# States and first batch loaded in F32 and cast on chip, attention one batch ahead, state rows inside the last batch

## The chip, the cores and the metric

The kernel runs on one core of a Trainium2 chip. A core has five engines that run their own instruction queues: TensorE (PE, with its weight loads shown as PEld), VectorE (DVE), ScalarE (ACT), GpSimd (POOL) and SyncE (SP). They meet only at semaphores, and 16 DMA engines move data between HBM and the on-chip memory. The metric is device time in microseconds of one execution of the whole program; lower is better.

## The reference

For each of 8 batches and 8 heads, 512 tokens `x` attend to 32 state rows, and the state rows attend back to the tokens. The two results are joined along the token axis (544 rows per batch), heads are put side by side into rows of 512, and a feed-forward layer with a maximum over three projections follows.

```python
scores = scale * np.matmul(x, state.transpose(0, 1, 3, 2))
a = softmax(scores)                      # over the 32 states
xread = np.matmul(a, state)              # (8, 8, 512, 64)
scores2 = scale * np.matmul(state, x.transpose(0, 1, 3, 2))
a2 = softmax(scores2)                    # over the 512 tokens
sread = np.matmul(a2, x)                 # (8, 8, 32, 64)
x = np.concatenate([xread, sread], axis=2).transpose(0, 2, 1, 3).reshape(4352, 512)
h = np.maximum(np.maximum(x @ w1, x @ w2), x @ w3)   # 512 -> 768
out = h @ w_out                                       # 768 -> 512
```

All inputs and the output are F32. The kernel computes its matmuls in bf16.

## The kernel before

Everything is unrolled and the order is written by hand: each engine executes its instructions in the order in which the source issues them, and the framework adds the semaphore waits from the tiles that are read and written. Buffers with a tag are shared: of the PSUM tag "two" (two banks each) there are two, of "pw" (one bank each) four.

Start. POOL issues all loads, and each of them casts F32 to bf16 on the way: the states (`st_sb`, two DMAs, L61), x of batch 0 (L71), six pieces of w1, w2, w3 (L81; half c=0 of the columns of all three, then half c=1), x of batches 1 and 2, `wout` (L91), and x of batches 3 to 7. The states are transposed on PE (L109) and copied into `bd` (L114 on DVE, L115 on ACT), where each head's transposed state lies once in the upper and once in the lower 64 partitions beside zeros, so that one matmul serves two token groups.

Attention of one batch is four pieces.

- `xt_piece` transposes x on PE into PSUM (`pxt`, L127) in two groups of eight, with a DVE copy to `xT` after each group (L130).
- `score_piece` multiplies with `bd` (`ps`, L136); ACT takes the exponential `e` (L141); DVE sums it (`den`, L143) and inverts (`rden`, L145); POOL multiplies to get the attention `a` (L147).
- `sread_piece` forms the state rows on PE (`psr`, L157 and L164) and normalises them on DVE (`rd`, `ats`, L170 and L171).
- `at_piece` transposes `a` on PE (`pat`, L180), copied by DVE to `aT` (L184).

The token rows never form xread. Instead `g_piece(b, u)`, for six u, multiplies the states of batch b with a sixth of the columns of w1, w2, w3 (`pg`, L197), and ACT casts the result to `G` (L202). `x_maxout(b, m)`, for six m of 128 hidden columns, multiplies `G` with `aT`: three projections of two matmuls each into three `pw` buffers (L212). ACT casts the first (`t0`, L216), DVE takes the two maxima (`t1`, L217; `ht`, L218). For m 0 to 2 it reads the columns of u 0 to 2, for m 3 to 5 those of u 3 to 5. `s_maxout(m)` does the same for the state rows of all batches, directly from the weights. `ffn_out(b, jj)` multiplies half of the tokens of `ht` with `wout` (`po`, 12 matmuls, L238), ACT copies to `osb` (L241), SP stores it (L248; the state rows in eight DMAs, L245).

Order. Attention of batch 0, its six g pieces, attention of batch 1. Then a loop over b, with six slots m: `x_maxout(b, m)` first, and after it what the slot holds. Slots 0, 2, 4, 5 hold the four attention pieces of batch b+2, slots 1 and 3 the two `ffn_out` of batch b-1, and every slot one g piece of batch b+1. After the loop come the six `s_maxout`, with the two `ffn_out` of batch 7 after the second and the fourth, and last the `ffn_out` of the state rows.

## Time and profile before

| | us |
|---|---|
| median of 3 runs | 213.42 (212.78 to 214.81) |
| profiled execution, device time | 215.94 |
| its span, first to last instruction | 214.1 |
| PE busy | 168.2 (79%) |
| DVE busy | 109.2 (51%) |
| ACT busy | 90.8 (42%) |
| POOL busy | 30.3 (14%) |
| PE weight loads (beside PE) | 87.9 (41%) |

The profile is of one execution. A group row gives the line, the engine, the operation, output and inputs by the program's names, the shapes, the count, then the busy time in us and the mean duration in ns, then the idle time of that engine just before and what ended it. A timeline row gives start and duration in us, engine, line and names, and in brackets how long the engine had been idle before and what released it. The chain that ended last is followed back from the last instruction, at each step to what released it; its rows are start, duration and piece. A DMA issue row gives the count, the size of one and the median time from issue to landing. Busy shares are means over stages with different limits, so the stretches of the span are to be read one by one. A run of matmuls is pipelined: the duration of a row holds the drain of the last one, so six matmuls of 512 columns show 1.47 us although the next instruction can start before that.

### The profile page before, as it was taken

To read this page: it belongs to the slowest core of one execution; us is meant where nothing else is said; L and a number is where in the kernel's file an instruction comes from. 1 tells how busy PE (TensorE), PEld (TensorE's weight loads), DVE (VectorE), ACT (ScalarE), POOL (GpSimd) and SP (SyncE) were. 2 spreads that over 40 slices of the span, in tenths; PEclk is the share of its full clock that TensorE was granted. 3 is DMA by queue.
4 is the path that set the end of the run, shared out by engine and by line. 5 is a ranking of instruction groups with operands and counts; after the bars stand their busy time and mean duration, and the time that the engine had idled before them with its cause. 6 is when DMAs were issued, how large, how long until landed. Compare 5 with 4: busy or idle time off the path is not lost.

```text
span 214.1 us, 3798 instructions
## 1 busy us (share of the span) xinstructions
PE 168.2 (79%) x1581; PEld 87.9 (41%) x1604; DVE 109.2 (51%) x170; ACT 90.8 (42%) x131; POOL 30.3 (14%) x31
## 2 busy tenths in 40 slices
PE   0452275589969996998799699978999999999970
PEld 0341125344434453444344344444444334456630
DVE  3334014456972776359645943595459338443330
ACT  2310081126544662654285327542865654342320
POOL 7944500300300300030003000300030000000000
PEclk9999999999999999999999969999999999999995
DMA  6999999910000120201022002100220210220223
GB/s 45 158 199 203 199 203 198 198 26 0 3 0 31 71 98 3 99 36 65 0 101 98 0 3 98 79 22 2 101 98 3 98 74 24 98 101 2 98 98 98
DMA packets 17056, 16.75 MB, mean 78 GB/s; under 512 B 2704, under 2 KB 14736, under 8 KB 17040
## 3 DMA queue, kind: packets, MB, share of 16 engines
q0 software_dynamic: 14352, 7.60, 26.0%
q1 hardware_dynamic: 2688, 8.91, 10.5%
q8 instruction: 12, 0.20, 0.4%
q14 instruction: 4, 0.03, 0.0%
HBM read 15.20 MB, written 8.91 MB: 113 GB/s over the span
## 4 chain that ended last, share of the span: by engine, by line
PE 50%; DVE 17%; ACT 9%; issue 8%; DMA 6%; POOL 5%; another core or an unknown queue 2%; DVEq 0%; ACTq 0%; POOLq 0%
PE pw L212 21%; PE po L238 20%; DVE t L217 6%; DMA w<-in_moe_w_dram 6%; DVE ht L218 4%; ACT G L202 4%; PE pg L197 3%; PE pxt L127 3%; ACT t L216 2%; DVE xT L130 2%; DVE rd L170 2%; POOL a L147 2%; PE ps L136 2%; ACT osb L241 2%
## 5 line engine op out<-in xcount | busy, mean ns | idle before, releaser
L212 PE MATMUL pw<-aT,G 128*128 128x512 bf16 x269 | 72.2, 395 | 2.7 <-issue 1.1
L217 DVE TENSOR_TENSOR t<-t,pw 128x512 bf16<-128x512 bf16 (+1 forms) x54 | 35.0, 648 | 56.1 <-ACT t L216 49.7
L202 ACT CAST G<-pg 128x768 bf16<-128x768 f32 x48 | 38.1, 801 | 46.0 <-PE pg L197 46.0
L238 PE MATMUL po<-wout,ht 128*128 128x512 bf16 x200 | 47.0, 383 | 0.2
L212 PEld LDWEIGHTS <-G 128*128 128x128 bf16 x288 | 25.4, 100 | 34.9 <-issue 13.1
L218 DVE TENSOR_TENSOR ht<-t,pw 128x512 bf16<-128x512 bf16 (+1 forms) x54 | 35.5, 658 | 5.6
L241 ACT COPY osb<-po 128x1024 f32<-128x1024 f32 x17 | 17.2, 1012 | 45.8 <-PE po L238 42.9
L216 ACT CAST t<-pw 128x512 bf16<-128x512 f32 (+1 forms) x54 | 31.0, 574 | 9.9 <-PE pw L212 9.8
L147 POOL TENSOR_TENSOR a<-e,rden 128x1024 bf16<-128x1024 bf16 x8 | 15.3, 1912 | 118.7 <-DVE rden L145 118.7
L238 PEld LDWEIGHTS <-ht 128*128 128x128 bf16 x204 | 20.2, 99 | 24.2 <-issue 1.3
L127 PE MATMUL pxt<-ident,x 128*128 128x128 bf16 x128 | 12.2, 252 | 13.0 <-DVE xT L130 11.1
L197 PE MATMUL pg<-w,bd 64*32 64x384 bf16 x384 | 18.3, 357 | 2.8 <-DVE ats L171 1.6
L130 DVE COPY xT<-pxt 128x1024 bf16<-128x1024 bf16 x16 | 11.0, 689 | 13.7 <-PE pxt L127 13.7
L127 PEld LDWEIGHTS <-x 128*128 128x128 bf16 x128 | 10.2, 114 | 16.4 <-issue 13.1
L180 PE MATMUL pat<-ident,a 128*128 128x128 bf16 x64 | 5.7, 242 | 10.4 <-POOL a L147 10.4
L197 PEld LDWEIGHTS <-bd 64*32 64x32 bf16 x384 | 5.9, 90 | 15.0 <-issue 13.0
L141 ACT ACTIVATE e<-ps 128x1024 bf16<-128x1024 f32 x8 | 8.2, 1023 | 8.8 <-PE ps L136 8.7
L143 DVE TENSOR_REDUCE den<-e 128x32 f32<-128x1024 bf16 x8 | 9.7, 1215 | 4.1 <-ACT e L141 3.9
L184 DVE COPY aT<-pat 128x1024 bf16<-128x1024 bf16 x8 | 5.5, 686 | 9.9 <-PE pat L180 9.9
L180 PEld LDWEIGHTS <-a 128*128 128x128 bf16 x64 | 4.7, 109 | 12.3 <-POOL a L147 10.9
L212 PE MATMUL pw<-ats,w 128*128 128x256 bf16 x72 | 8.5, 273 | 0.0
L71 POOL DMA_DIRECT2D x<-in_x_dram x8 | 7.1, 884 | 6.4 <-DMA w<-in_moe_w_dram 5.9
(29 smaller groups left out, 68.6 us busy)
## 6 DMA issues: line engine op xcount, KB each, us to landing
out_dram<-osb SPq DMA_DIRECT2D x16, 512.0 KB, 2.6
x<-in_x_dram POOLq DMA_DIRECT2D x8, 512.0 KB, 20.2
w<-in_moe_w_dram POOLq DMA_DIRECT2D x6, 384.0 KB, 10.5
wout<-in_moe_w_out_dram POOLq DMA_DIRECT2D x1, 768.0 KB, 19.0
out_dram<-osb SPq DMA_DIRECT2D x8, 64.0 KB, 1.7
st<-in_state_dram POOLq DMA_DIRECT2D x2, 128.0 KB, 3.7
```

What stands on the lines that cost most here:

```text
L127: nc.tensor.transpose(pxt[:, h, jj, :], x_sb[b][:, h, 2 * jj:2 * jj + 2, :].rearrange("p j d -> p (j d)"), ident)
L130: nc.vector.tensor_copy(out=xT[b][:, 4 * g:4 * g + 4], in_=pxt[:, 4 * g:4 * g + 4])
L147: nc.gpsimd.tensor_mul(out=a[b].rearrange("p j h n -> p (j h) n"), in0=e[b].rearrange("p j h n -> p (j h) n"), in1=rden.rearrange("p j h - ...
L180: nc.tensor.transpose(pat[:, q * 512 + j * 128:q * 512 + j * 128 + 128], a[b][:, j, 4 * q:4 * q + 4, :].rearrange("p h n -> p (h n)"), ident)
L197: nc.tensor.matmul(pg[32 * hh:32 * hh + 32, r, 0:384], bd[64 * r:64 * r + 64, b, h, r, :], w_sb[c][64 * r:64 * r + 64, hh, k * 384:(k + 1) ...
L202: nc.scalar.copy(out=G[b][:, :, u * 384:(u + 1) * 384], in_=pg[:, :, 0:384])
L212: nc.tensor.matmul(p[:, 0:n], lhs(i, m, k), rhs(k), start=(k == 0), stop=(k == nk - 1))
L216: nc.scalar.copy(out=t0[:, 0:n], in_=pw[0][:, 0:n])
L217: nc.vector.tensor_max(t1[:, 0:n], t0[:, 0:n], pw[1][:, 0:n])
L218: nc.vector.tensor_max(ht[b][:, m, :], t1[:, 0:n], pw[2][:, 0:n])
L238: nc.tensor.matmul(po[:, c, :], ht[b][:, m, j * 128:(j + 1) * 128], wout_sb[:, m, :], start=(m == 0), stop=(m == NM - 1))
L241: nc.scalar.copy(out=o, in_=po)
```

## The change

Loads: the states go as one F32 DMA on ACT's queue, x of batch 0 as two F32 DMAs (four heads each) on SP's queue; DVE and ACT cast them to bf16. POOL's queue at the start holds the six weight pieces, x of batch 1 and `wout`; x of batch b+2 is issued at the top of loop b. The states lie in the partitions in another order, 16 consecutive rows each, and `bd` is filled by `bd_piece`, four copies for batch 0 and four for batches 1 to 7, the latter issued after the scores of batch 0. The transposed states wait for it in two "pw" buffers.

Attention: all 16 transposes of a batch come before the two copies to `xT`, which are ACT's (for batch 0 the second is DVE's). The multiply of batch 0 is DVE's. The loop carries attention of batch b+1 in slots 0, 1, 3, 4, and `ffn_out` of batch b-1 stands first in slots 2 and 5. In loop 7 each slot holds one `s_maxout`. At the end come `ffn_out` for half of batch 7, for the state rows, and two of one token group each, whose copy is split between ACT and DVE. Four of the eight stores of the state rows are POOL's.

```diff
--- before.py
+++ after.py
@@ -56,22 +56,22 @@
     ctx.enter_context(tc.manual_schedule())
 
 
-    st_sb = data.tile([128, 16, 2, D], BF16, name="st")
-    for q in range(2):
-        nc.gpsimd.dma_start(
-            out=st_sb.rearrange("p (b q) c d -> p b q c d", q=2)[:, :, q, 0, :],
-            in_=state[:, 4 * q:4 * q + 4].rearrange("b h n d -> (h n) b d"),
-        )
+    def x_rows(b):
+        return x[b].rearrange("h (p j) d -> p h (j d)", j=J)
+
+    x_sb = [data.tile([128, H, J, D], BF16, name=f"x{b}") for b in range(B)]
+    st_f = data.tile([128, 16, D], F32, name="stf")
+    nc.scalar.dma_start(
+        out=st_f, in_=state.rearrange("b h n d -> (b h n) d").rearrange("(p t) d -> p t d", t=16))
+    x_f = [data.tile([128, 4, J * D], F32, name=f"xf{g}") for g in range(2)]
+    for g in range(2):
+        nc.sync.dma_start(out=x_f[g], in_=x_rows(0)[:, 4 * g:4 * g + 4, :])
+
     ident = const.tile([128, 128], BF16, name="ident")
     make_identity(nc, ident)
 
-    x_sb = [data.tile([128, H, J, D], BF16, name=f"x{b}") for b in range(B)]
-
     def load_x(b):
-        nc.gpsimd.dma_start(
-            out=x_sb[b].rearrange("p h j d -> p h (j d)"),
-            in_=x[b].rearrange("h (p j) d -> p h (j d)", j=J),
-        )
+        nc.gpsimd.dma_start(out=x_sb[b].rearrange("p h j d -> p h (j d)"), in_=x_rows(b))
 
     w_sb = [wpool.tile([128, NHP, HALF], BF16, name=f"w{c}") for c in range(2)]
     wout_sb = wpool.tile([128, NM, d_model], BF16, name="wout")
@@ -83,14 +83,10 @@
                 in_=w.rearrange("(kk p) f -> p kk f", p=128)[:, :, c * 384:(c + 1) * 384],
             )
 
-    load_x(0)
     load_w(0)
     load_w(1)
     load_x(1)
-    load_x(2)
     nc.gpsimd.dma_start(out=wout_sb, in_=moe_w_out.rearrange("(kk p) f -> p kk f", p=128))
-    for b in range(3, B):
-        load_x(b)
 
     ones = const.tile([128, 64], BF16, name="ones")
     nc.vector.memset(ones, 1.0)
@@ -102,17 +98,25 @@
     ats = data.tile([128, NHP, B * Ns], BF16, name="ats")
 
 
-    nc.vector.tensor_copy(out=st_sb[:, :, 1, :], in_=st_sb[:, :, 0, :])
-    for g in range(2):
-        pt = pp.tile([128, 2048], BF16, tag="two", name="pt")
-        for t in range(8):
-            nc.tensor.transpose(
-                pt[:, 128 * t:128 * t + 128],
-                st_sb[:, 8 * g + t].rearrange("p c d -> p (c d)"), ident)
-        src = pt[:, 0:1024].rearrange("p (bh n) -> p bh n", n=Ns)
-        dst = bd[:, 4 * g:4 * g + 4].rearrange("p b h c n -> p (b h) c n")
-        nc.vector.tensor_copy(out=dst[0:64, :, 0, :], in_=src[0:64])
-        nc.scalar.copy(out=dst[64:128, :, 1, :], in_=src[64:128])
+
+    st_sb = data.tile([128, 16, 2, D], BF16, name="st")
+    nc.vector.tensor_copy(out=st_sb[:, :, 0, :], in_=st_f)
+    nc.scalar.copy(out=st_sb[:, :, 1, :], in_=st_f)
+    pt = [pp.tile([128, 8, 128], BF16, tag="pw", bufs=4, name=f"pt{k}") for k in range(2)]
+    for t in range(16):
+        nc.tensor.transpose(pt[t // 8][:, t % 8, :], st_sb[:, t].rearrange("p c d -> p (c d)"), ident)
+    nc.vector.tensor_copy(out=x_sb[0][:, 0:4].rearrange("p h j d -> p h (j d)"), in_=x_f[0])
+    nc.scalar.copy(out=x_sb[0][:, 4:8].rearrange("p h j d -> p h (j d)"), in_=x_f[1])
+
+    def bd_piece(b0, b1):
+        for k in range(2):
+            for c, copy in enumerate((nc.vector.tensor_copy, nc.scalar.copy)):
+                r = slice(64 * c, 64 * c + 64)
+                dst = bd[r, b0:b1, :, c, :].rearrange("p b h (g t) -> p (b h) g t", t=16)
+                copy(out=dst[:, :, :, 8 * k:8 * k + 8],
+                     in_=pt[k][r, :, 16 * b0:16 * b1].rearrange("p t (k g) -> p k g t", g=2))
+
+    bd_piece(0, 1)
 
 
     xT, e, a, aT, G, ht = {}, {}, {}, {}, {}, {}
@@ -121,13 +125,14 @@
 
         xT[b] = work.tile([128, H, 2, 128], BF16, tag="xT", name="xT")
         pxt = pp.tile([128, H, 2, 128], BF16, tag="two", name="pxt")
-        for g in range(2):
-            for h in range(4 * g, 4 * g + 4):
-                for jj in range(2):
-                    nc.tensor.transpose(
-                        pxt[:, h, jj, :],
-                        x_sb[b][:, h, 2 * jj:2 * jj + 2, :].rearrange("p j d -> p (j d)"), ident)
-            nc.vector.tensor_copy(out=xT[b][:, 4 * g:4 * g + 4], in_=pxt[:, 4 * g:4 * g + 4])
+        for h in range(H):
+            for jj in range(2):
+                nc.tensor.transpose(
+                    pxt[:, h, jj, :],
+                    x_sb[b][:, h, 2 * jj:2 * jj + 2, :].rearrange("p j d -> p (j d)"), ident)
+        second = nc.vector.tensor_copy if b == 0 else nc.scalar.copy
+        nc.scalar.copy(out=xT[b][:, 0:4], in_=pxt[:, 0:4])
+        second(out=xT[b][:, 4:8], in_=pxt[:, 4:8])
 
     def score_piece(b):
         ps = pp.tile([128, J, H, Ns], F32, tag="two", name="ps")
@@ -144,7 +149,8 @@
         rden = work.tile([128, J, H], F32, tag="rden", name="rden")
         nc.vector.reciprocal(out=rden, in_=den)
         a[b] = work.tile([128, J, H, Ns], BF16, tag="a", name="a")
-        nc.gpsimd.tensor_mul(
+        mul = nc.vector.tensor_mul if b == 0 else nc.gpsimd.tensor_mul
+        mul(
             out=a[b].rearrange("p j h n -> p (j h) n"),
             in0=e[b].rearrange("p j h n -> p (j h) n"),
             in1=rden.rearrange("p j h -> p (j h)").unsqueeze(2).to_broadcast((128, J * H, Ns)))
@@ -204,7 +210,7 @@
 
     def maxout(b, m, n, lhs, rhs, nk):
         if m == 0:
-            ht[b] = work.tile([128, NM, n], BF16, tag="ht", name="ht")
+            ht[b] = work.tile([128, NM, n], BF16, tag="ht", bufs=3, name="ht")
         pw = []
         for i in range(3):
             p = pp.tile([128, 512], F32, tag="pw", bufs=4, name=f"pw{i}")
@@ -230,57 +236,63 @@
                lambda k: ats[:, k, :], NHP)
 
 
-    def ffn_out(b, jj):
+    def ffn_out(b, j0, j1):
         po = pp.tile([128, 2, d_model], F32, tag="two", name="po")
-        for c in range(2):
-            j = 2 * jj + c
+        for j in range(j0, j1):
             for m in range(NM):
-                nc.tensor.matmul(po[:, c, :], ht[b][:, m, j * 128:(j + 1) * 128], wout_sb[:, m, :],
+                nc.tensor.matmul(po[:, j - j0, :], ht[b][:, m, j * 128:(j + 1) * 128], wout_sb[:, m, :],
                                  start=(m == 0), stop=(m == NM - 1))
+        n = j1 - j0
         o = work.tile([128, 2, d_model], F32, tag="osb", bufs=3, name="osb")
-        nc.scalar.copy(out=o, in_=po)
+        if n == 1:
+            nc.scalar.copy(out=o[:, 0, 0:256], in_=po[:, 0, 0:256])
+            nc.vector.tensor_copy(out=o[:, 0, 256:512], in_=po[:, 0, 256:512])
+        else:
+            nc.scalar.copy(out=o, in_=po)
         if b == "s":
             for k in range(B):
                 r0 = k * SP + S
-                nc.sync.dma_start(out=out[r0:r0 + Ns, :],
-                                  in_=o[32 * (k % 4):32 * (k % 4) + 32, k // 4, :])
+                (nc.sync if k < 4 else nc.gpsimd).dma_start(
+                    out=out[r0:r0 + Ns, :], in_=o[32 * (k % 4):32 * (k % 4) + 32, k // 4, :])
             return
         nc.sync.dma_start(
-            out=out[b * SP:b * SP + S, :].rearrange("(p j) f -> p j f", j=J)[:, 2 * jj:2 * jj + 2, :],
-            in_=o)
-
-
-    def attention(b):
-        return [lambda: xt_piece(b), lambda: score_piece(b), lambda: sread_piece(b),
-                lambda: at_piece(b)]
-
-    for f in attention(0):
-        f()
-    for u in range(NG):
+            out=out[b * SP:b * SP + S, :].rearrange("(p j) f -> p j f", j=J)[:, j0:j1, :],
+            in_=o[:, 0:n, :])
+
+
+    xt_piece(0)
+    score_piece(0)
+    bd_piece(1, B)
+    sread_piece(0)
+    for u in range(3):
         g_piece(0, u)
-    for f in attention(1):
-        f()
+    at_piece(0)
+    for u in range(3, NG):
+        g_piece(0, u)
 
     for b in range(B):
+        if b + 2 < B:
+            load_x(b + 2)
         slots = [[] for _ in range(NM)]
-        if b > 0:
-            slots[1].append(lambda: ffn_out(b - 1, 0))
-            slots[3].append(lambda: ffn_out(b - 1, 1))
-        if b + 2 < B:
-            for f, m in zip(attention(b + 2), (0, 2, 4, 5)):
-                slots[m].append(f)
         if b + 1 < B:
+            for f, m in ((xt_piece, 0), (score_piece, 1), (sread_piece, 3), (at_piece, 4)):
+                slots[m].append(lambda f=f: f(b + 1))
             for u in range(NG):
                 slots[u].append(lambda u=u: g_piece(b + 1, u))
+        else:
+            for m in range(NM):
+                slots[m].append(lambda m=m: s_maxout(m))
+        if b > 0:
+            slots[2].insert(0, lambda: ffn_out(b - 1, 0, 2))
+            slots[5].insert(0, lambda: ffn_out(b - 1, 2, 4))
         for m in range(NM):
             x_maxout(b, m)
             for f in slots[m]:
                 f()
-    for m in range(NM):
-        s_maxout(m)
-        if m in (1, 3):
-            ffn_out(B - 1, m // 2)
-    ffn_out("s", 0)
+    ffn_out(B - 1, 0, 2)
+    ffn_out("s", 0, 2)
+    ffn_out(B - 1, 2, 3)
+    ffn_out(B - 1, 3, 4)
 
 
 # ---- launch: one core; inputs and outputs as the reference has them ----
```

## The prediction

> **What bounds the kernel now.** I read the time in stretches first, cut where a new batch's first maxout matmul starts, then the chain that ended last, then the timeline inside single stretches. The stretches (length, then busy time of PE, PEld, DVE, ACT, POOL; the last three columns are granted clock, DMA share, GB/s):
>
> ```profile
> 0.00:41.40 41.40, 16.14 (x224) 12.14 (x226) 12.84 (x20) 9.93 (x12) 18.84 (x25) 1.00 1.27 174
> 41.40:58.80 17.40, 16.02 (x162) 7.75 (x163) 11.77 (x18) 7.94 (x12) 1.91 (x1) 1.00 0.18 25
> 99.30:119.60 20.30, 17.94 (x194) 9.05 (x190) 12.47 (x20) 10.47 (x15) 1.91 (x1) 1.00 0.13 52
> 119.60:141.50 21.90, 19.51 (x193) 9.44 (x188) 12.38 (x20) 10.56 (x15) 1.91 (x1) 0.92 0.12 49
> 161.80:177.60 15.80, 15.55 (x114) 6.05 (x108) 8.34 (x14) 9.37 (x14) 0.00 (x0) 1.00 0.16 67
> 177.60:207.20 29.60, 29.16 (x173) 16.32 (x168) 14.14 (x26) 10.10 (x17) 0.00 (x0) 1.00 0.18 72
> 207.20:214.10 6.90, 0.03 (x1) 0.00 (x0) 0.00 (x0) 1.01 (x1) 0.00 (x0) 0.67 0.30 76
> ```
>
> PE is busy 17.94 of 20.3 us in a full loop and 29.16 of 29.6 us in the end piece: there PE is the bound. In the first 41.4 us it works 16.1: the head, 19% of the span, is a wait. Its longest pieces in the chain, and DVE's rows of batch 0:
>
> ```profile
> 7.66 12.24 DMA w<-in_moe_w_dram
> 21.06 1.60 issue
> 23.56 1.93 POOL a L147
> 27.94 2.95 ACT G L202 x4
> 38.19 1.92 POOL a L147
> ```
>
> ```profile
> 15.80 1.22 DVE L143 TENSOR_REDUCE den<-e 128x32 f32<-128x1024 bf16 x1 [1.97 <-ACT e L141]
> 17.05 0.35 DVE L145 RECIPROCAL rden<-den 128x32 f32<-128x32 f32 x1
> 17.35 0.96 DVE L170 RECIPROCAL rd<-psr 128x128 f32<-128x128 f32 x1
> 18.34 0.29 DVE L171 TENSOR_TENSOR ats<-psr,rd 128x128 bf16<-128x128 f32 x1
> ```
>
> The multiply of batch 0 (L147) has its input at 17.4, but stands on POOL behind x loads that wait for older loads, and starts at 23.56. Then come six G casts and the whole attention of batch 1, its multiply at 38.19, before any maxout at 41.4. In the loop, two waits make up nearly all of the 2.36 us in which PE idles:
>
> ```profile
> 82.67 0.61 PE L127 MATMUL pxt<-ident,x 128*128 128x128 bf16 x8 [1.77 <-DVE xT L130]
> ...
> 98.99 0.35 PE L197 MATMUL pg<-w,bd 64*32 64x384 bf16 x8 [0.33 <-DVE ats L171]
> ```
>
> **The change part by part: the head.** POOL's queue, the first copies, ACT's groups and the DMA issues price it:
>
> ```profile
> 1.24 1.94 POOL L61 DMA_DIRECT2D st<-in_state_dram  x2 [0.79 <-POOLq L298]
> ...
> 3.70 0.89 POOL L71 DMA_DIRECT2D x<-in_x_dram  x1
> 4.58 4.58 POOL L81 DMA_DIRECT2D w<-in_moe_w_dram  x6
> ...
> 14.33 0.88 POOL L71 DMA_DIRECT2D x<-in_x_dram  x1 [1.08 <-DMA w<-in_moe_w_dram]
> 16.27 0.87 POOL L71 DMA_DIRECT2D x<-in_x_dram  x1 [1.06 <-DMA w<-in_moe_w_dram]
> ```
>
> ```profile
> 6.21 0.43 DVE L105 COPY st<-st 128x1024 bf16<-128x1024 bf16 x1 [3.12 <-DMA st<-in_state_dram]
> ...
> 6.70 1.89 PE L109 MATMUL pt<-ident,st 128*128 128x128 bf16 x16 [6.70 <-DVE st L105]
> 7.76 0.68 DVE L114 COPY bd<-pt 64x1024 bf16<-64x1024 bf16 x1 [1.13 <-PE pt L109]
> 8.48 1.01 ACT L115 COPY bd<-pt 64x1024 bf16<-64x1024 bf16 x1 [6.25 <-DVE bd L114]
> ```
>
> ```profile
> L202 ACT CAST G<-pg 128x768 bf16<-128x768 f32 x48 | 38.1, 801 | 46.0 <-PE pg L197 46.0
> ...
> L141 ACT ACTIVATE e<-ps 128x1024 bf16<-128x1024 f32 x8 | 8.2, 1023 | 8.8 <-PE ps L136 8.7
> ```
>
> ```profile
> out_dram<-osb SPq DMA_DIRECT2D x16, 512.0 KB, 2.6
> ...
> out_dram<-osb SPq DMA_DIRECT2D x8, 64.0 KB, 1.7
> st<-in_state_dram POOLq DMA_DIRECT2D x2, 128.0 KB, 3.7
> ```
>
> Loads: two releases 1.94 us apart (14.33, 16.27) give one w piece, 384 KB written and 768 KB read: about 395 KB read per us, 1.3 us per 512 KB. The states and the two halves of x[0] are three F32 pieces of 512 KB. Issued at about 0.8 by ACT and SP, the first lands 2.6 us later (as the output row), the others 1.3 us apart: 3.4, 4.7, 6.0 if nothing shares. POOL loses the state and x[0] issues (1.94 + 0.89), so w starts at 1.75 instead of 4.58, and with most of the 3.7 us of a small POOL load its data flow from about 4.2. From there I halve the rate of x[0], since all loads use the same 16 DMA engines: some 0.75 MB are left, and the second half lands at 8.0. Ends: 6.0, and 10 if it gets a third.
>
> That the queues share is a rule of the Trainium skill too ("DMA: Bandwidth & Descriptors", section "Issuing engines are not separate DMA queues"): loads from several engines interleave on the same DMA engines, and only issue time is saved. It speaks against a gain from the new queues as such; without it the sum would be 2 us lower. No run before the change has two loads side by side.
>
> From 8.0: ACT casts heads 4 to 7 (1.0, as L115) to 9.05; the second eight transposes (half of 1.89) to 10.1, with four small bd copies of batch 0 beside them; ACT's xT copy 1.0, DVE's beside it, to 11.1; scores 1.0, 12.1; exp 1.02, 13.15; den 1.22 and rden 0.35, 14.75; the multiply, now on DVE, 1.2 (1024 elements as den; ends 0.7 and 1.9), 16.0. DVE's two F32 casts are over by then (0.7 each; ends 0.43 and 1.22, L105 and L143).
>
> Then bd of the seven other batches, 896 columns in four strided copies, DVE and ACT in turn. ACT's first bd copy began at 8.48, just as DVE's into the other half of bd ended (7.76 + 0.68), so I let the four go one after the other: 0.8, 0.95, 0.8, 0.95, to 19.5. Ends: 2.7 us less if both run at once, 3 more if the scattered pattern halves the rate. It is a new wait: on ACT all six G casts stand behind the last copy, and DVE's rd and ats (1.25, done 19.8) hold the PSUM buffer that the second pg needs.
>
> G casts of 0.80, 0.85 with the hand-over since only two PSUM buffers turn: from 19.5, three by 22.0; at_piece 21.25 to 22.3 (1.05, slow PE); g 3 to 5 until 24.25. The first maxout starts at **24.3** for 41.4. The weights stay hidden: 1.5 MB + 6 x 0.77 MB at 395 KB per us is 15.6 us, from 2.5 on about 18, and g 3 asks at 22.3. Cover 4 us; beyond it the end moves one for one. x[1] follows 2.6 us later, 20.7; PE asks at 27. So the six x loads taken out of the start cost nothing; later they go out one per loop, two loops ahead (0.88 us on POOL ahead of a multiply whose input comes 9 us into the loop).
>
> **Loop 0.** 17.4 before:
>
> ```profile
> 41.41 2.34 PE L212 MATMUL pw<-aT,G 128*128 128x512 bf16 x5 [0.22 <-issue]
> ...
> 45.39 1.01 PE L127 MATMUL pxt<-ident,x 128*128 128x128 bf16 x8 [0.78 <-DVE xT L130]
> ...
> 49.63 1.47 PE L212 MATMUL pw<-aT,G 128*128 128x512 bf16 x6
> ```
>
> The xt wait goes (0.78); the at_piece may come 0.2 late: **16.8**. Five maxout matmuls take 2.34 us at first, six take 1.47 from 49.6 on: PE runs at half speed for the first 8 us of dense work. I keep that, since the loop again follows an idle head. The Trainium skill ("TensorE: Matmul & The Clock Gate", section "Part 1: The HAM clock gate (the "warmup" mystery)") ends the half clock after about 3.4 us of sustained activity; by that the loop would be some 1 us shorter, but the trace shows 8.
>
> **Loops 1 to 6.** DVE's rows for what moves:
>
> ```profile
> L217 DVE TENSOR_TENSOR t<-t,pw 128x512 bf16<-128x512 bf16 x48 | 32.5, 677 | 49.4 <-ACT t L216 43.0 <-PE pw L212 6.1
> L130 DVE COPY xT<-pxt 128x1024 bf16<-128x1024 bf16 x16 | 11.0, 689 | 13.7 <-PE pxt L127 13.7
> ...
> L217 DVE TENSOR_TENSOR t<-t,pw 128x256 bf16<-128x256 bf16 x6 | 2.5, 420 | 6.7 <-ACT t L216 6.7
> ```
>
> Work 17.94 each. Gone: the 1.77 wait (all 16 transposes now stand ahead of both copies) and the 0.33 at pg. Late next: both xT copies are on ACT, 2 x 1.0 for DVE's 2 x 0.69, and the scores moved up a slot. Behind the transposes PE has pg and x_maxout 1 (0.35 and 1.47, 1.6 without the drains) to cover 0.15 + 2.0: a wait of 0.6 at the scores. On ACT the G cast, t0 of maxout 1 and exp stand behind the copies: 0.25 at the next pg (its buffer), 0.1 at maxout 2 (third pw). At g 4, psr is released late by ats: 0.3. Sum 1.25, loop **19.2** (ends: 18.0, all hidden; 20.3, as now). The path from the scores over exp, den, rden and POOL's 1.9 needs about 6 us and has 8.9 (two maxouts, one ffn_out, sread): hidden. Loop 6 now carries attention 7: six loops, 115.2. Before, 58.8 to 177.6 was 118.8, with five such loops and one of 15.8, so of the head's 17 us loop 6 gives 3.4 back.
>
> **End piece.** s_maxout moves into loop 7: the same matmuls, 29.16. Each slot asks DVE for 2 x 0.79 + 2 x 0.47 = 2.5 us (0.68 and 0.42 with hand-over) in PE's 2.6, with two ffn_out as slack: 0.3 of waits, **29.5** for 29.6.
>
> ```profile
> 207.27 1.01 ACT L241 COPY osb<-po 128x1024 f32<-128x1024 f32 x1 [3.09 <-PE po L238]
> 208.31 3.63 SPq L245 DMA_DIRECT2D out_dram<-osb  x8
> ```
>
> Now 6.9 us follow the last matmul: copy 1.0, eight issues 3.63, landing 1.7, rest 0.5. After, two single ffn_out (1.34 each, half of 2.7) stand behind the s one, so its copy and four SP issues (0.45 each) are over 0.3 after the last matmul. POOL's four at 0.88 reach +2.0 and land by +4.7 (3.7 from the last issue's start, as the states; with 1.7, +2.9). SP's last, behind the split copies, lands at +3.5. With the rest, **5.2** (ends 4.0 and 5.8).
>
> **Sum.** 24.3 + 16.8 + 115.2 + 29.5 + 5.2 = 191.0 for the span of 214.1. This execution took 215.94, 1.84 outside the span and 2.5 above the median of the runs, 213.42; 1.6 of that is the stretch of 21.9 at clock 0.92, which my sum has not. So 191.0 + 1.84, less the other 0.9: **192 us**.
>
> **The rivals.**
> - Head later: x[0] gets less than half, or the scattered bd copies run at half rate. For it: nothing in this trace loads on two queues or writes such a pattern. Against: the 4 us of cover touch w alone. 192 + 2 + 3 = **197**.
> - ACT's order becomes the loop's bound: its work is only 12.5 of 19 us, but what stands behind the xT copies comes late in each loop. No gain in six loops, 6 x 1.1: **198.6**.
> - All hidden: bd copies side by side (-2.7), loops of 18.2 (-6): **183.3**. Against: the 8.48 start, and the transposes that waited for a copy of the other half.
> - The other side, slower: with attention one batch ahead, each at_piece waits for its POOL multiply. Seven loops have to lose 21.4 us, 3.1 each, so it decides once scores to pat takes 12 us instead of 6; at 13 the time is 192 + 7 x 4.1 = **221**. Against: no wait at pat in the loops of this trace.
> - No change: x[1], behind six w pieces, lands at 44 instead of 20.7, which costs loop 0 17 us, and the loops stay at 19.9: 192 + 17 + 4 = **213**. The load rate speaks against it.
>
> **How the numbers follow.** Forecast 0.57, head later 0.16, ACT's order 0.12, all hidden 0.10, slower 0.03, no change 0.02. Range 185 to 199: the ends of head (-2.7, +5) and loops (-7, +6.6) seldom fall together; left out are the last three cases, 0.15. About 1% is what a measurement of this kernel can tell from no change. Faster 0.95, same 0.02, slower 0.03.
>
> **What would show it.** First maxout near 24.3, batch 0's last G casts at 20 to 25 behind a bd copy; a multiply on DVE near 15; loops of 19.2 with a PE wait at the scores on ACT's xT and none at the transposes; 5 us behind the last matmul, ended by a POOL transfer. I am wrong if the first maxout starts after 29, or loops take over 20.3 or under 18.

## The result and the profile after

| us | before | after |
|---|---|---|
| median of 4 runs each, on one chip | 214.04 (212.78 to 214.81) | 189.95 (189.44 to 190.21) |
| ratio | | 0.888 (95% interval 0.882 to 0.893) |
| profiled execution, its span | 215.94, 214.1 | 189.44, 187.6 |

The changed kernel is 11% faster. The forecast was 192 us, two above. Some executions of the kernel before took over 1.5% longer than its fastest one; the ratios, here and below, leave such executions out, the medians do not. The stretches of the changed kernel, cut like those of before at the first maxout matmul of a batch (length, then busy time of PE, PEld, DVE, ACT and POOL; the last three columns are granted clock, DMA share and GB/s): the head, loop 0, a full loop, the end piece, and what follows the last matmul.

```profile
0.00:24.04 24.04, 10.39 (x145) 7.11 (x145) 11.53 (x16) 11.39 (x15) 8.18 (x15) 1.00 1.16 213
24.04:39.32 15.28, 14.20 (x172) 6.93 (x165) 9.84 (x16) 10.62 (x16) 2.80 (x2) 1.00 0.48 62
77.39:96.43 19.04, 18.31 (x197) 9.08 (x189) 11.16 (x17) 12.21 (x18) 2.80 (x2) 1.00 0.37 84
153.55:182.83 29.28, 29.06 (x176) 16.30 (x168) 13.29 (x25) 11.32 (x19) 1.24 (x3) 1.00 0.19 76
182.83:187.60 4.77, 0.01 (x1) 0.00 (x0) 0.42 (x1) 0.37 (x1) 0.83 (x2) 0.84 0.64 196
```

PE's work of the head is 10.4 us for 16.1 before, because batch 1's attention has left it, and the head has shrunk by 17.4. A full loop went from 20.30 to 19.04 and PE is busy for 96% of it. The last stretch lost 2.1 of 6.9. The first part of the profile's page says the same of the whole:

```profile
PE 163.5 (87%) x1604; PEld 84.8 (45%) x1604; DVE 103.3 (55%) x161; ACT 106.2 (57%) x151; POOL 28.0 (15%) x31
```

The terms of the forecast beside what they became; a full loop is the mean of six:

| us | forecast | measured |
|---|---|---|
| head, to the first maxout | 24.3 | 24.04 |
| loop 0 | 16.8 | 15.28 |
| loops 1 to 6 | 115.2 (19.2 each) | 114.23 (19.04 each) |
| end piece | 29.5 | 29.28 |
| after the last matmul | 5.2 | 4.77 |
| span | 191.0 | 187.6 |

Inside the head, the timeline (start and duration in us, engine, line, names; in brackets the idle time before, and the releaser):

```profile
4.82 1.04 ACT L104 CAST st<-stf 128x1024 bf16<-128x1024 f32 x1 [2.14 <-DMA stf<-in_state_dram]
...
6.06 0.69 DVE L108 CAST x<-xf 128x1024 bf16<-128x1024 f32 x1 [0.18 <-DMA xf<-in_x_dram]
...
7.78 1.04 ACT L109 CAST x<-xf 128x1024 bf16<-128x1024 f32 x1 [1.91 <-DMA xf<-in_x_dram]
...
9.95 1.01 ACT L134 COPY xT<-pxt 128x1024 bf16<-128x1024 bf16 x1 [0.68 <-PE pxt L130]
10.99 0.69 DVE L135 COPY xT<-pxt 128x1024 bf16<-128x1024 bf16 x1 [2.78 <-ACT xT L134]
...
15.29 1.23 DVE L153 TENSOR_TENSOR a<-e,rden 128x1024 bf16<-128x1024 bf16 x1
16.44 2.07 DVE L116 COPY bd<-pt 64x896 bf16<-64x896 bf16 x2
17.55 1.90 ACT L116 COPY bd<-pt 64x896 bf16<-64x896 bf16 x2 [3.93 <-DVE bd L116]
...
19.47 2.38 ACT L208 CAST G<-pg 128x768 bf16<-128x768 f32 x3
```

The states have landed at 4.8, the first half of x[0] at 6.0 and the second at 7.78, and ACT casts that one. The two xT copies of batch 0 read different halves of `pxt`, on two engines, yet DVE starts at 10.99, as ACT ends (9.95 + 1.01). The multiply is DVE's, at 15.29. The large bd copies run from 16.44 to 19.45. ACT's first one (from 17.55) starts when DVE's first one ends, but DVE's second one, to 18.51, runs beside it, both into `bd`. Behind the last of them stand the G casts. This is the new wait of the head.

In a full loop:

```profile
79.97 1.47 PE L218 MATMUL pw<-aT,G 128*128 128x512 bf16 x6
...
80.69 1.02 ACT L135 COPY xT<-pxt 128x1024 bf16<-128x1024 bf16 x1
...
81.60 0.82 ACT L208 CAST G<-pg 128x768 bf16<-128x768 f32 x1
81.77 0.63 PE L141 MATMUL ps<-bd,xT 128*128 128x64 bf16 x16 [0.33 <-ACT xT L135]
...
91.86 0.36 PE L203 MATMUL pg<-w,bd 64*32 64x384 bf16 x8 [0.33 <-DVE ats L177]
```

No transpose waits any more. Where nothing waits, what follows six maxout matmuls starts 1.30 us after them (89.62 to 90.92 in this loop); the scores start 1.80 after (79.97 to 81.77), because ACT's second xT copy ends at 81.71. So this wait costs 0.5. With 0.1 at the next pg, 0.1 at the third pw of maxout 2 and 0.4 at the pg behind `ats`, by the same reading of starts, PE loses 1.1 us per loop.

At the end:

```profile
181.32 1.75 SPq L255 DMA_DIRECT2D out_dram<-osb  x4
181.59 2.07 POOL L255 DMA_DIRECT2D out_dram<-osb  x4 [36.41 <-ACT osb L251]
...
183.17 0.96 SPq L258 DMA_DIRECT2D out_dram<-osb  x2
183.32 0.42 DVE L249 COPY osb<-po 128x256 f32<-128x256 f32 x1 [0.87 <-DMA out_dram<-osb]
```

POOL has issued its four stores by 183.66, 0.52 us each; SP issues the last one at 183.7 to 184.13. The profile's page gives 3.0 us from the issue to the landing of such a 256 KB store and 2.3 for POOL's of 64 KB:

```profile
out_dram<-osb SPq DMA_DIRECT2D x2, 256.0 KB, 3.0
```

### The profile page after: what moved, and what is told of

Read it like the earlier page. It is cut to its first block, busy times and chain, and to the rows that moved or that the text cites. A ratio compares the mean times of both kernels' runs of the same rounds, so it can differ in the third digit from the quotient of the medians.

```text
span 187.6 us, 3845 instructions
## 1 busy us (share of the span) xinstructions
PE 163.5 (87%) x1604; PEld 84.8 (45%) x1604; DVE 103.3 (55%) x161; ACT 106.2 (57%) x151; POOL 28.0 (15%) x31
## 4 chain that ended last, share of the span: by engine, by line
PE 54%; ACT 18%; DVE 16%; issue 6%; DMA 4%; SPq 0%; DVEq 0%; ACTq 0%
PE pw L218 22%; PE po L243 22%; ACT G L208 7%; PE pg L203 4%; PE pxt L130 4%; DVE rd L176 4%; ACT xT L135 4%; DVE t L223 4%; DMA xf<-in_x_dram 3%; DVE ht L224 3%; ACT xT L134 2%; ACT t L222 2%; ACT osb L251 2%; DVE ats L177 1%; DVE den L148 1%
## 5 line engine op out<-in xcount | busy, mean ns | idle before, releaser
L251 ACT COPY osb<-po 128x1024 f32<-128x1024 f32 x16 | 16.2, 1012 | 37.3 <-PE po L243 37.3
L153 POOL TENSOR_TENSOR a<-e,rden 128x1024 bf16<-128x1024 bf16 x7 | 13.3, 1904 | 116.9 <-DVE rden L150 116.9
L203 PEld LDWEIGHTS <-bd 64*32 64x32 bf16 x384 | 6.6, 90 | 17.3 <-issue 9.8
L134 ACT COPY xT<-pxt 128x1024 bf16<-128x1024 bf16 x8 | 8.1, 1012 | 5.0 <-PE pxt L130 5.0
L130 PE MATMUL pxt<-ident,x 128*128 128x128 bf16 x128 | 9.5, 231 | 0.1
L130 PEld LDWEIGHTS <-x 128*128 128x128 bf16 x128 | 8.5, 104 | 2.0 <-ACT x L109 0.4
L141 PE MATMUL ps<-bd,xT 128*128 128x64 bf16 x128 | 5.6, 199 | 3.7 <-ACT xT L135 2.3
L141 PEld LDWEIGHTS <-xT 128*128 128x128 bf16 x128 | 5.1, 101 | 6.9 <-issue 4.3
L218 PEld LDWEIGHTS <-w 128*128 128x128 bf16 x72 | 7.0, 98 | 2.4 <-issue 0.3
L176 DVE RECIPROCAL rd<-psr 128x128 f32<-128x128 f32 x8 | 7.6, 949 | 0.0
```

The source lines that it names most:

```text
L130: nc.tensor.transpose(pxt[:, h, jj, :], x_sb[b][:, h, 2 * jj:2 * jj + 2, :].rearrange("p j d -> p (j d)"), ident)
L134: nc.scalar.copy(out=xT[b][:, 0:4], in_=pxt[:, 0:4])
L153: mul(out=a[b].rearrange("p j h n -> p (j h) n"), in0=e[b].rearrange("p j h n -> p (j h) n"), in1=rden.rearrange("p j h -> p (j h)").unsqu ...
L176: nc.vector.reciprocal(out=rd, in_=psr[:, 128:256])
L203: nc.tensor.matmul(pg[32 * hh:32 * hh + 32, r, 0:384], bd[64 * r:64 * r + 64, b, h, r, :], w_sb[c][64 * r:64 * r + 64, hh, k * 384:(k + 1) ...
L218: nc.tensor.matmul(p[:, 0:n], lhs(i, m, k), rhs(k), start=(k == 0), stop=(k == nk - 1))
```

## The experiments

The theory from this profile: the head is the landing of x[0] plus a fixed chain, the loop is PE's work plus the waits of the order, and both parts of the change (earlier loads, attention one batch ahead) pay by the sums above. Rivals: the loads' own queues were worth little, the change of order alone brought all, or the engines that take turns in the head do so for another reason than the one given. Baselines are runs of the kernel before on the same chip: 214.78 us for the first four experiments, 215.8 for the next four, 214.28 for the last four (experiments 9 to 12).

**1. Loads of the states and x[0] back on POOL.** The changed kernel, with these loads casting in the DMA again, ahead of the weights:

```diff
-    st_f = data.tile([128, 16, D], F32, name="stf")
-    nc.scalar.dma_start(
+    st_f = data.tile([128, 16, D], BF16, name="stf")
+    nc.gpsimd.dma_start(
...
-    for g in range(2):
-        nc.sync.dma_start(out=x_f[g], in_=x_rows(0)[:, 4 * g:4 * g + 4, :])
...
+    load_x(0)
     load_w(0)
     load_w(1)
...
-    nc.vector.tensor_copy(out=x_sb[0][:, 0:4].rearrange("p h j d -> p h (j d)"), in_=x_f[0])
-    nc.scalar.copy(out=x_sb[0][:, 4:8].rearrange("p h j d -> p h (j d)"), in_=x_f[1])
```

> The changed kernel with the states and x[0] loaded by POOL with the cast again, ahead of the weights; all else as changed. Theory (the gain of the head comes from the emptied POOL queue and from attention 1 leaving the head, the F32 loads on other queues are worth little): POOL issues x[0] at about 2.2, it lands 6.5 us later as before the change, at 8.7, and needs no cast, so the second eight transposes start at about 8.9 as in the changed kernel (8.87). The weights start 1.7 us later but stay hidden. First maxout 24 to 25, time 190 to 191. Rival (the F32 loads on their own queues carry the head): x[0] lands at 10 or later, first maxout over 26, time over 192.

Measured 192.82 us (191.58 to 193.41), ratio 0.905 (0.896 to 0.913), 2.9 above the change and 2.1 above its second measurement (experiment 12). PE's timeline:

```profile
10.77 1.89 PE L125 MATMUL pxt<-ident,x 128*128 128x128 bf16 x16 [2.54 <-DMA x<-in_x_dram]
```

The load was issued at 2.47, 1.2 us earlier than in the kernel before, and was no sooner usable: 10.77. The first maxout came at 26.79, 2.75 behind the first profile of the changed kernel and 2.04 behind its second (24.75). The theory's 190 to 191 fell and its rival held: F32 loads on their own queues are worth 2.0 to 2.8 us. The edit moves the cast into the DMA together with the queue, so it does not show which of the two it is. All else that the head gained (41.4 to 26.8) came without them.

**2. Only the later x loads moved, in the kernel before.** The loads of x[3] to x[7] go out one per loop, so that POOL is free when the multiply of batch 0 has its input:

```diff
-    for b in range(3, B):
-        load_x(b)
...
     for b in range(B):
+        if b + 3 < B:
+            load_x(b + 3)
```

> The kernel before with one edit: x of batches 3 to 7 is issued one per loop (x of b+3 at the top of loop b), not at the start. Theory (POOL's queue held the multiply of batch 0): the multiply starts at 17.5 instead of 23.56, first maxout at 35.5 instead of 41.4, nothing else moves, time 214 - 6 = 208. Rival (the weights bind instead, or x comes late in the loops): first maxout at 39 or later, time 212 or more.

```profile
17.50 1.91 POOL L144 TENSOR_TENSOR a<-e,rden 128x1024 bf16<-128x1024 bf16 x1 [3.84 <-DVE rden L142]
```

Measured 207.85 us (206.94 to 211.66), ratio 0.975 (0.963 to 0.986). The multiply starts at 17.50 instead of 23.56, right behind `rden`, and the first maxout at 35.72 instead of 41.4. Theory held for the head: one multiply behind POOL's queue of loads cost 5.7 us of it. "Nothing else moves" did not hold in the profiled executions, whose spans differ by 8.9 us (205.2 for 214.1): loop 0 is 1.6 shorter (15.83), and no loop is 1.6 longer than the others, as the one of 21.9 was.

**3. Only the order moved, in the kernel before.** Attention of batch 1 leaves the head and each loop carries batch b+1 in the slots of the changed kernel:

```diff
-    for f in attention(1):
-        f()
...
-            slots[1].append(lambda: ffn_out(b - 1, 0))
-            slots[3].append(lambda: ffn_out(b - 1, 1))
-        if b + 2 < B:
-            for f, m in zip(attention(b + 2), (0, 2, 4, 5)):
+            slots[2].append(lambda: ffn_out(b - 1, 0))
+            slots[5].append(lambda: ffn_out(b - 1, 1))
+        if b + 1 < B:
+            for f, m in zip(attention(b + 1), (0, 1, 3, 4)):
                 slots[m].append(f)
```

> The kernel before with one edit: attention one batch ahead (attention b+1 in slots 0, 1, 3, 4 of loop b, ffn_out in slots 2 and 5, attention 1 no longer ahead of the loop). Theory: attention 1 (10.5 us) leaves the head, first maxout at 31; loop 6 now carries attention 7 and goes from 15.8 to 20.3; loops stay at 20.3; time 214 - 10.5 + 4.5 = 208. Rival (one batch ahead is too late, at_piece waits for POOL's multiply): loops over 21, time 212 or more.

Measured 212.95 us (211.48 to 214.76), ratio 0.997 (0.991 to 1.003): no change. The head did shrink, by 10.2 us to 31.21, and in the span of the profiled executions 1.2 of it was left (212.9 for 214.1). Its stretches (columns as above; head, loops 1 to 4):

```profile
0.00:31.21 31.21, 10.49 (x145) 7.10 (x145) 8.64 (x13) 7.97 (x10) 16.82 (x24) 1.00 1.21 165
...
48.88:69.07 20.19, 18.18 (x196) 9.04 (x189) 13.69 (x21) 9.73 (x15) 1.91 (x1) 1.00 0.07 28
69.07:91.44 22.37, 19.77 (x196) 9.45 (x189) 12.55 (x19) 10.57 (x16) 1.91 (x1) 0.92 0.12 48
91.44:112.24 20.80, 18.20 (x197) 9.04 (x189) 12.54 (x19) 10.48 (x16) 1.91 (x1) 1.00 0.13 52
112.24:134.57 22.33, 19.73 (x196) 9.67 (x189) 12.55 (x19) 10.46 (x16) 1.91 (x1) 0.92 0.12 48
```

Two things ate it. Loop 6, 15.8 us in the kernel before because it had no attention to carry, now has the whole 20.79: 5.0 given back, as must be when a batch is only moved. And loops 1 to 5 sum to 106.5 for 103.0: the usual one takes 20.80. PE's and DVE's timeline in the third of the rows above:

```profile
70.38 0.61 PE L127 MATMUL pxt<-ident,x 128*128 128x128 bf16 x8
73.26 0.80 PE L127 MATMUL pxt<-ident,x 128*128 128x128 bf16 x8 [2.27 <-DVE xT L130]
73.99 0.52 PE L197 MATMUL pg<-w,bd 64*32 64x384 bf16 x8
74.44 1.89 PE L212 MATMUL pw<-aT,G 128*128 128x512 bf16 x4
```

```profile
71.13 0.69 DVE L217 TENSOR_TENSOR t<-t,pw 128x512 bf16<-128x512 bf16 x1 [3.30 <-ACT t L216]
71.92 0.69 DVE L218 TENSOR_TENSOR ht<-t,pw 128x512 bf16<-128x512 bf16 x1
72.53 0.68 DVE L130 COPY xT<-pxt 128x1024 bf16<-128x1024 bf16 x1
```

The second eight transposes wait for DVE's copy of the first eight, which stands behind the two maxima of slot 0. These now come later, since an `ffn_out` closes the loop before and its osb copy runs on ACT ahead of `t0`: the wait grew from 1.77 to 2.27. After it, in two of seven loops, PE runs at half speed: four maxout matmuls take 1.89, where six take 1.47 at full speed. That makes the loop 1.55 longer and its granted clock 0.92. So the theory's 208 fell.

**4. Both in the kernel before.** Edits 2 and 3 together:

> The kernel before with both edits: x of b+3 in loop b, and attention one batch ahead. Theory (the two parts of the head add up): first maxout at 25, time 214 - 6 - 6 = 202; what is left to the changed kernel (12 us) is the loops (seven times 1.25), the end (2) and the loads and copies of the head (1). Rival (they hide each other): 205 or more.

Measured 207.16 us (203.72 to 208.75); its four executions lie too far apart for a ratio. One took 203.72 at a mean granted clock of 0.991, three took 207.07 to 208.75 at 0.977, the first of them the profiled one. Head, and a loop with half speed (the next one takes 20.79):

```profile
0.00:25.37 25.37, 10.49 (x144) 7.11 (x145) 8.82 (x13) 7.97 (x10) 13.32 (x20) 1.00 1.17 154
61.39:83.81 22.42, 19.82 (x197) 9.57 (x189) 12.55 (x19) 10.57 (x16) 2.79 (x2) 0.92 0.33 71
```

The head is within 1.3 us of the changed kernel's with neither hardware queues nor F32 loads, and yet the span, 205.3, is 17.7 longer. Most of the difference is in the loops: loop 0 is 0.6 longer, loop 1 1.1, loops 2 to 6 1.76 each (20.80 against 19.04), together 10.5; the two half-speed loops add 3.2, the end from loop 7 on 2.7 (36.77 against 34.05), the head 1.3. The sum, 17.7, leaves nothing over. Without the two half-speed loops the profiled time of 207.07 would be 203.9, close to the 203.72 of the execution at the higher clock. The median met the rival's number (205 or more), by a cause that neither had named; the execution at the higher clock lies between the two.

**5. The transposes in two groups again, in the changed kernel:**

```diff
-        for h in range(H):
+        for g in range(2):
+            for h in range(4 * g, 4 * g + 4):
...
-        second = nc.vector.tensor_copy if b == 0 else nc.scalar.copy
-        nc.scalar.copy(out=xT[b][:, 0:4], in_=pxt[:, 0:4])
-        second(out=xT[b][:, 4:8], in_=pxt[:, 4:8])
+            second = nc.vector.tensor_copy if b == 0 and g else nc.scalar.copy
+            second(out=xT[b][:, 4 * g:4 * g + 4], in_=pxt[:, 4 * g:4 * g + 4])
```

> The changed kernel with the transposes of x in two groups of eight again, a copy after each group (the copies stay on the same engines as in the change). Theory (the order of transposes and copies is what the loops gained): the second group waits about 1.3 us for ACT's copy of the first in every loop, the scores no longer wait 0.5, loops of 19.8 instead of 19.04, seven times 0.75, time 190 + 5 = 195; if PE falls back to half speed after the wait, as after some xT waits of the kernel before, 1.6 more for each time. Rival (only the engine of the copies matters, not the order): loops within 0.2 of 19.04, time 190.

Measured 195.63 us (195.17 to 195.93), ratio 0.914 (0.909 to 0.920), 5.7 above the change.

```profile
83.85 0.61 PE L131 MATMUL pxt<-ident,x 128*128 128x128 bf16 x8 [1.10 <-ACT xT L135]
```

The wait at the transposes is back at 1.10, the loops take 19.62, and the head ends at 25.40. Theory held: that all transposes stand ahead of the copies is worth 0.58 us in each loop and 0.5 of the head's 1.4 (x[0] was there at 8.66 for 7.78). Of the 1.76 by which experiment 4's loops were longer, the other 1.18 lies between 20.80 and 19.62: there the copies are on ACT, not behind DVE's maxima, and `ht` has a third buffer. The two were not tried apart.

**6 and 7. Who takes turns with whom in the head.** The prediction laid the turns of DVE and ACT in `bd_piece` to the tile that both write, `bd`. The other theory: they take turns on the PSUM tile that both read. In experiment 6 the copies are crossed, so that DVE and ACT read different PSUM tiles at a time and still write the one `bd`:

```diff
-        for k in range(2):
+        for i in range(2):
             for c, copy in enumerate((nc.vector.tensor_copy, nc.scalar.copy)):
+                k = (i + c) % 2
```

In experiment 7 batch 0's transposes go to two PSUM tiles of one bank each, while both copies still write one `xT`:

```diff
+        if b == 0:
+            ph = [pp.tile([128, 4, 2, 128], BF16, tag="pw", bufs=4, name=f"ph{k}") for k in range(2)]
...
+            nc.scalar.copy(out=xT[b][:, 0:4], in_=ph[0])
+            nc.vector.tensor_copy(out=xT[b][:, 4:8], in_=ph[1])
+            return
```

> The changed kernel with one edit in the bd copies: ACT takes the second half of the transposed states first, DVE the first half, then they change over. Theory A (two engines take turns on one PSUM tile, and the two halves are two tiles): ACT's first large bd copy starts together with DVE's (16.4), the last ends 1.0 earlier (18.5), the first G cast starts 1.0 earlier, and the first maxout about 0.4 (the second pg still waits for ats, or for the first cast): time 189.6. Theory B, the one in the prediction (they take turns because both write bd): ACT still starts when DVE's copy ends, nothing moves.

> The changed kernel with one edit: for batch 0 the transposed x goes into two PSUM tiles of one bank each instead of one tile of two banks. Theory A (two engines take turns on one PSUM tile even in different banks): ACT's and DVE's xT copies of batch 0 now run side by side, the scores start 0.7 earlier (from 11.7 to 11.0), first maxout at 23.3, time 189.3. Theory B (they take turns because both write xT): DVE's copy still starts when ACT's ends, nothing moves.

The timeline of the crossed copies, then that of the two tiles:

```profile
14.95 0.90 ACT L117 COPY bd<-pt 64x896 bf16<-64x896 bf16 x1
...
17.73 2.07 DVE L117 COPY bd<-pt 64x896 bf16<-64x896 bf16 x2
18.84 0.90 ACT L117 COPY bd<-pt 64x896 bf16<-64x896 bf16 x1 [3.00 <-DVE bd L117]
```

```profile
10.47 1.01 ACT L134 COPY xT<-ph 128x1024 bf16<-128x1024 bf16 x1
10.71 0.69 DVE L135 COPY xT<-ph 128x1024 bf16<-128x1024 bf16 x1 [2.28 <-PE ph L131]
```

Crossed, ACT copies as soon as exp is done, ahead of DVE, and its second copy (18.84 to 19.74) runs beside DVE's second (about 18.8 to 19.8), both into `bd`. With two PSUM tiles DVE's copy runs beside ACT's, both into `xT`. So sharing the tile that is written makes no turns, and sharing the PSUM tile does, also for different banks of it. The times show no gain: 190.16 us (189.32 to 191.64), ratio 0.890 (0.884 to 0.896), and 190.11 (189.39 to 190.85), ratio 0.889 (0.884 to 0.894). In the profiled executions that is in part the head's first term. x[0] was there at 9.08 and 8.96, not at 7.78; counted from there to the first maxout, the head took 15.8 and 14.7 us, for 16.26 in the first profile of the change and 15.89 in its second. So the two tiles are worth about 1 us of the chain or somewhat more; some tenths are PE's, whose second eight transposes took 0.62 there, and 0.96 in the second profile. Crossing is worth 0.1 to 0.4: the first G cast comes 1.0 earlier (10.69 behind the landing for 11.69), but the next pg waits for that cast.

**8. The second xT copy on DVE in every batch:**

```diff
-        second = nc.vector.tensor_copy if b == 0 else nc.scalar.copy
+        second = nc.vector.tensor_copy
```

> The changed kernel with the second xT copy on DVE in all batches. Theory: DVE's copy comes after ACT's first and after ht of maxout 0, so the scores start at the same time (0.05 earlier), but ACT is free 1 us sooner for the G cast, t0 and exp; the waits at the next pg (0.14) and at maxout 2 (0.06) go: loops of 18.8, time 188.3. Rival (DVE, with 0.7 us more per loop, is late with the maxima): loops of 19.04 or more, time 190 or more.

```profile
80.71 0.68 DVE L135 COPY xT<-pxt 128x1024 bf16<-128x1024 bf16 x1
...
81.42 0.63 PE L141 MATMUL ps<-bd,xT 128*128 128x64 bf16 x16
```

Measured 187.98 us (187.36 to 189.08), ratio 0.880 (0.874 to 0.886). The copy ends at 81.39 and the scores start 1.58 behind maxout 1 (79.84) instead of 1.80. ACT's G cast and `t0`, no longer behind that copy, are earlier too, and the loops take 18.63. Theory held: 0.4 us of the loop stood behind ACT's second copy.

**9, 10 and 12. The multiply of batch 0 on POOL; all eight state-row stores on SP; the changed kernel once more.** The first two change one line each of the changed kernel, and the third is the yardstick beside them. The multiply:

```diff
-        mul = nc.vector.tensor_mul if b == 0 else nc.gpsimd.tensor_mul
+        mul = nc.gpsimd.tensor_mul
```

The stores:

```diff
-            (nc.sync if k < 4 else nc.gpsimd).dma_start(
+            nc.sync.dma_start(
```

> The changed kernel with the multiply of batch 0 back on POOL, whose queue is empty by then. Theory (the head's chain is exp, den, rden, the large bd copies, the G casts, and a stands in DVE's order without need): POOL starts the multiply at about 15.3 and ends at 17.2, well before at_piece asks for it (21); DVE's bd copies start 1.2 earlier, and all G casts with them: first maxout 1.2 earlier counted from the landing of x[0] (16.3 us after it in the changed kernel, 15.1 here), time 188.8. Rival (POOL's multiply of 1.9 and its queue set the end): at_piece waits for POOL, first maxout no earlier, time 190 or more.

> The changed kernel with all eight stores of the state rows on SP. Theory (SP's last store of batch 7 ends the kernel, POOL's four are done before): SP needs 4 x 0.44 more ahead of it, the end comes 1.3 to 1.7 us later, 6.1 to 6.5 us after the last matmul instead of 4.8, time 191.3 to 191.7. Rival, the prediction's (POOL's stores end last): the end does not come later than 4.8 us after the last matmul, time 190 or less.

> The changed kernel once more, beside the others. Loops of 19.04 as before. If the spread of its time comes from the landing of x[0], the first maxout lies 16.3 us behind the start of ACT's cast of x[0], as in its first profile (7.78 and 24.04), wherever that is; time 189.4 to 190.8.

The changed kernel took 190.69 us (190.17 to 191.8), ratio 0.893 (0.889 to 0.897). In its profile x[0] is cast at 8.86 and the first maxout starts at 24.75, 15.89 later and not the expected 16.3: twelve of the sixteen score matmuls took 0.52 us for 0.82 there, so PE was faster early in this head. Loop 0 took 15.98, the loops 19.04.

With the multiply on POOL: 190.14 us (189.14 to 190.37), ratio 0.889 (0.884 to 0.894). The bd copies start at 16.12, beside the multiply (16.36 to 18.27, which the pat of 20.81 does not wait for), and landing to first maxout is 14.94. The 0.95 us that this gains over 15.89 appear in the head; loop 0 gives 0.3 back, and the medians differ by 0.55. The expected 188.8 was not reached.

With all stores on SP: 192.55 us (192.13 to 193.05), ratio 0.901 (0.897 to 0.906).

```profile
183.16 3.62 SPq L255 DMA_DIRECT2D out_dram<-osb  x8
...
186.88 0.88 SPq L258 DMA_DIRECT2D out_dram<-osb  x2
```

Here the last two stores are ready (DVE's last copy ends at 185.58) and stand behind the eight. SP's queue ends the kernel, 6.13 us after the last matmul for 4.85 in the yardstick, as the theory had it: POOL's four stores are worth 1.3 us and are not the end. The medians differ by 1.9; of the rest, 0.4 lies ahead of the end in the profiles (first maxout 0.3 later, loop 0 0.1 longer).

**11. Edits 6, 7, 8 and 9 together,** in the changed kernel:

> The changed kernel with four edits together: bd copies crossed, xT of batch 0 from two PSUM tiles, second xT copy on DVE in all batches, multiply of batch 0 on POOL. Theory (they lie on different pieces of the same chain and of the loop): 0.4 + 0.8 + 2.0 + 1.2 = 4.4 us, time 185.6, loops of 18.6, first maxout 14 us after the landing of x[0]. Rival (the weights or ats bind next in the head): the three edits of the head give 1 us or less together, time 187 or more.

Measured 184.86 us (184.27 to 185.78), ratio 0.865 (0.861 to 0.870): the fastest kernel here, 3% below the change. Theory held. Head, loop 0 and a full loop:

```profile
0.00:21.98 21.98, 10.26 (x145) 7.11 (x145) 9.94 (x15) 11.40 (x15) 10.16 (x16) 1.00 1.13 212
21.98:36.96 14.98, 14.37 (x173) 6.87 (x165) 10.66 (x17) 9.80 (x15) 2.80 (x2) 1.00 0.68 97
73.20:91.80 18.60, 18.16 (x189) 9.00 (x188) 11.77 (x18) 11.39 (x16) 2.80 (x2) 1.00 0.40 86
```

x[0] is cast at 8.52, so the chain behind it takes 13.46 instead of 15.89 to 16.26. ACT's last large bd copy ends at 16.83, and the first G cast starts at 16.85 instead of 19.47. Alone, counted in the same way against 15.89, crossing gave 0.1, the two tiles 1.2 and the multiply 0.95, together 2.2; at once they gave 2.4. In the chain the three edits add up, within the few tenths by which PE's speed in the head differs. In the medians of single edits they hardly show: x[0] landed at 8.7 to 9.1 there, and loop 0 moved by some tenths.

## Why the prediction was right

**The head (24.3; 24.04).** The chain has the links of the forecast, but the sum hit by errors that cancel: the landing was 0.2 early, DVE's xT copy ran behind ACT's and not beside it (0.7), and the bd copies took 3.0 for 3.5. Landing of x[0] was forecast for 8.0 by halving its rate beside the weights from 4.2 on, and was 7.78; without sharing it would have been 6.0. The way there was another one. The three pieces landed at 4.8, 6.0 and 7.78 for 3.4, 4.7 and 8.0: the first two were 1.3 to 1.4 late already, and the last came 1.8 behind the second, not 3.3. So half a rate is not what the trace shows. That the loads were later than alone fits the rule of the Trainium skill ("DMA: Bandwidth & Descriptors", section "Issuing engines are not separate DMA queues") that loads from several engines share the same DMA engines. That only issue time is saved fits less well: in experiment 1 the load issued at 2.47 was usable at 10.77 and the head 2.0 to 2.8 us longer, of which the later issue (2.47 for 0.74 to 1.73) explains 0.7 to 1.7. What is left can also be the cast in the DMA. In nine executions with these loads the cast of the second half began at 7.78 to 9.08, eight times at 8.5 or later, so some of the hit at 24.04 is luck too: 24.75, as in experiment 12, was more likely.

**The bd copies: size roughly right, cause wrong.** The prediction took them strictly in turn, 3.5 us, because both engines write `bd`; they took 3.0. A DVE copy took 1.04 for 0.8, so all four in turn would have been 4.0; but DVE's second runs beside ACT's first, which that cause does not allow. (The xT copies of batch 0, which share a written tile too, the prediction set side by side.) Experiments 6 and 7 showed that it is the PSUM tile. The Trainium skill ("PSUM — Partial Sum Buffer", section "PSUM bank collisions raise a hardware error") forbids two engines one bank in the same 32 partitions and allows different banks. That agrees: in experiments 6 and 7 DVE and ACT read different banks side by side once these are different tiles. So the turns are not a matter of banks. In the traces they are waits for the other engine's copy (`<-ACT xT L134` above), and another division into tiles removes them.

**Loop 0 (16.8; 15.28): the term that was mis-sized.** The prediction kept the 8 us of half speed that the kernel before showed, and put some 1 us on a shorter ramp; the loop was 1.5 shorter. PE's timeline in the changed kernel:

```profile
22.99 1.11 PE L203 MATMUL pg<-w,bd 64*32 64x384 bf16 x16 [0.33 <-DVE aT L190]
...
24.04 2.24 PE L218 MATMUL pw<-aT,G 128*128 128x512 bf16 x6
...
26.11 1.06 PE L130 MATMUL pxt<-ident,x 128*128 128x128 bf16 x16
```

Sixteen transposes in 1.06 us are full speed (the sixteen of the states took 1.87 at 6.03), 2.1 us into the loop. The granted clock of this profile reads 1.00 all through the head and loop 0, so here only the durations show the half speed. In the profile of experiment 12 the column has it too; its loop 0:

```profile
24.75:40.73 15.98, 14.90 (x173) 7.27 (x165) 9.85 (x16) 10.63 (x16) 2.80 (x2) 0.91 0.43 57
```

In narrower windows it is 0.50 until 27.6 and 1.00 from 27.8, 3 us into the loop, and the first six maxout matmuls took 2.74. So the 15.28 is 0.7 better than that by an earlier end of the half clock, which is luck. The rule that the prediction set aside, an end of the half clock after about 3.4 us of sustained work ("TensorE: Matmul & The Clock Gate" of the Trainium skill, section "Part 1: The HAM clock gate (the "warmup" mystery)"), was nearer: the g matmuls ahead of the loop keep PE at work from 22.99 on, 3.1 us before 26.11, and in experiment 12 from 23.70 on, 4.0 us before the clock rose. Nor do 8 us follow from an idle head: experiment 2 has the order of the kernel before, and its transposes are at full speed 2.5 us after the first maxout (35.72 to 38.19).

**Loops 1 to 6 (19.2; 19.04).** Work 17.94 and waits of 1.25 were forecast, and 1.1 of waits found, at the four places named: 0.5, 0.1, 0.1 and 0.4 for 0.6, 0.25, 0.1 and 0.3. The forecast did not ask what the new order would do without the new place of the copies. Experiment 3 did: with the old copies it brings nothing. The loops' gain belongs to the transposes and copies, with a part that may be the third buffer of `ht`; without it, of 16 us of shorter head (41.40 to 25.37) 7.6 reached the median in experiment 4, and 11.1 the one execution at the higher clock.

**The end (34.7; 34.05).** The end piece came out as forecast. Behind the last matmul the sum was near (5.2, 4.77) and its story wrong: a POOL store issues in 0.52 us, not the 0.88 of a casting load, and lands in 2.3, not 3.7, so POOL is done first and SP's last 256 KB store ends the kernel, as experiment 10 shows. The split copies ahead of that store take turns too: DVE's half starts at 182.03, as ACT's ends (181.62 + 0.37), and both read one `po`. What two tiles would bring there was not tried.

**The rivals.** All hidden (183.3) was nearest to becoming true: its two conditions, bd copies side by side and a loop of about 18, are what experiment 11 builds, and it took 184.86. ACT's order as the loop's bound was partly there: 0.4 us of each loop, by experiment 8.

## What to carry to other kernels

When a stage is moved out of the head, ask what stands ahead of its first copy in the place where it now runs: the move alone gave nothing here (experiment 3), and the loops stopped giving its gain back once the transposes and copies had moved too. Two engines that read different halves of one PSUM tile take turns; give each its own tile or let them start on different ones. An edit that is worth less than the scatter of an earlier event (here 1.3 us in one landing) shows in the trace before it shows in the time, so judge it by the distance between two events, against more than one execution of the kernel that it changes.

## What was unexpected

**Half speed in the middle of a loop.** In experiments 3 and 4, and in the kernel before, PE dropped to half speed (granted clock 0.50) within 2 us after some of the waits at the second eight transposes, for about 3.4 us, with 1.6 us lost each time:

```profile
123.26 0.61 PE L127 MATMUL pxt<-ident,x 128*128 128x128 bf16 x8 [1.77 <-DVE xT L130]
...
124.34 2.34 PE L212 MATMUL pw<-aT,G 128*128 128x512 bf16 x5 [0.20 <-issue]
```

This is the kernel before, in the loop of 21.9 us. Waits of 1.77 and 2.27 could do it; the 1.10 of experiment 5 and the shorter ones of the changed kernel never did in a profile. Experiment 2 had waits of 1.77 and no such loop. Why one wait of a length does it and the next does not stays open; that a shorter wait ends it is what the profiles show, not a test of the threshold.

**The landing of the same load moved by 1.3 us** between executions (7.78 to 9.08) although it was issued at the same time. Nothing here says why; it hides edits of the head that are worth less.
